# Block sums beside the keys, longer constant products, an added mask and a new order in a sparse-attention and mixture-of-experts kernel

## Chip, cores and metric

The kernel runs on one core of a Trainium2 chip. The metric is device time in microseconds (us). A kernel's time is the median of its runs. The profiled span of a run is some 1.6 us shorter than its time (184.9 against 186.49 in the profiled run of the kernel before).

A run is labelled slow when it is over 1.5% above the fastest run of the same kernel, fast otherwise.

## The reference

There are four sequences (batch entries) of 768 positions. Eight attention heads of 64 channels look at a local window of 31 keys and at 24 block summaries: the maximum of each block's 32 keys and the mean of its values. Then the whole sequence goes to one of eight experts.

```python
k_sum = k.reshape(B, H, nb, block, D).max(axis=3)       # block = 32, nb = 24
v_sum = v.reshape(B, H, nb, block, D).mean(axis=3)
mask_l = np.abs(pos[:, None] - pos[None, :]) < window   # window = 16
scores_s = scale * q @ k_sum.T + np.log(block)          # (einsum, shortened)
a = softmax([where(mask_l, scale * q @ k.T, -1e9), scores_s])
x = a @ [v, v_sum]                                      # -> (B, 768, 512)
# ... mixture of experts, one choice per sequence
logits = x.mean(axis=1) @ w_gate
e = argmax(logits)                                      # one of 8
out = softmax(logits)[e] * (relu(x @ w1[e]) @ w2[e])    # w1 512x1024, w2 1024x512
```

## The kernel before

The kernel carries its own list scheduler. It estimates when each operation can start, picks one by priority, and so fixes the order of instructions on each engine before anything runs. While sequence b+1 is in attention, TensorE works on the expert of sequence b. Three parts matter here.

**The filler.** TensorE's granted clock falls to half for some stretches (0.50 from 30.0 to 40.2 us in the kernel before). The scheduler is written to prevent that: wherever it expects TensorE to have little to do, it puts products of constants into the list. They count as busy in the profiles (22.8 of TensorE's 171.4 busy us in the kernel before).

```python
def keep_warm(self, t, op):
    end = self.work[-1][1]
    idle = t - end
    if t < self.FILL_TO:                       # 45.0
        unit = 0.107 if t < 6.5 else 0.0555
        n = max(0, int((idle - 0.1) / unit))
        past = ...                             # weighted busy time of the last SPAN = 3 us
        thin = self.DENSE * self.SPAN - past - n * unit     # DENSE = 0.5
        if t > 7.0 and thin > 0:
            more = min(int(thin / unit) + 1, 10)
            n += more
    ...
    if self.fill(n): ...

def fill(n):
    ...
    for _ in range(n):
        nc.tensor.matmul(idle[:, 0:128], lhsT=idle_in, rhs=idle_in, start=True, stop=True)
```

**The block sums.** The keys of one query block (96 rows) and the 24 block maxima give 120 rows of scores in one tile `aT`. For the values, the sums of 32 rows are made by a product with a block indicator (`bind`). In sequences 0 to 2 they stay in a tile of their own, `vs`, and a second group of products adds their part. In sequence 3 they are copied by DMA into rows 96 to 119 beside every block's values, and one product with 120 rows does both.

```python
APART = (0, 1, 2)
def av(pr, hf):
    ...
    rows = KW if b in APART else NR            # 96 or 120
    for hh in range(2):
        for jj in range(NH):
            nc.tensor.matmul(ops[...], lhsT=aT[0:rows, hh, ...], rhs=vb[0:rows, pr, j, hh, :], ...)
    if b not in APART:
        return
    for hh in range(2):
        for s in range(NS):                    # six more products per half
            nc.tensor.matmul(ops[:, hh, s, :], lhsT=aT[KW:NR, hh, ...],
                             rhs=vsps[b % 2][KW:NR, pr, hh, :], start=False, ...)
def mk(pr, hf):                                # the mask, on VectorE, after the exponential
    nc.vector.tensor_tensor(out=aT[0:NR], in0=aT[0:NR], in1=mask[...], op=ALU.mult)
```

**The gate and the loads.** The mean of sequence b gives its expert's number, and only then can the two weight matrices be loaded (1 MB each). For sequence 0, w1 comes in two halves, so that the expert can start on the first one. The output leaves through three tiles.

```python
def w1f(half):
    fs = slice(half * (F // 2), (half + 1) * (F // 2)) if b == 0 else slice(0, F)
    nc.gpsimd.dma_start(sb["w1"][:, :, fs], moe_w1[ds(sb["e"], 1)]...)
# letters: A = ScalarE, D = VectorE, per sequence and pair of heads
EK = ("AAAA", "DAAD", "DAAD", "DDDD")          # key copies
EQ = ("ADAD", "AADD", "DDDD", "DADD")          # query copies
KB = ("ADDA", "ADAD", "ADAD", "DAAD")          # key maxima
CAST = ("DDAD", "DDDD", "DDDD", "DDDD")        # casts of the values
o_pool = ctx.enter_context(tc.tile_pool(name="o", bufs=3))
```

The softmax here doesn't subtract the row's maximum and nothing guards it: scores larger than these inputs give would overflow.

## Time and profile before

| | before |
|---|---|
| time, median of 3 runs | 188.2 us (187.96 to 188.72) |
| span of the profiled run | 184.9 us |
| start to gate 0 | 41.3 us |
| gate 0 to first expert product | 9.7 us |
| first expert product to gate 3 | 96.5 us |
| gate 3 to end | 37.4 us |

These four stretches add up to the span. "Gate b" is the start of the gate products of sequence b. Three lines of the page of the kernel before help to read it. The first two are rows of 40 slices of 4.6 us: TensorE's busy tenths, and the mean busy share of the DMA engines. The third is the filler: busy time in us, then nanoseconds of one instruction.

```profile
PE   7898973999999989999999999999999999899991
...
DMA  5999999604999999799999999944100039990052
...
L1031 PE MATMUL third<-idle_in 128*128 128x128 bf16 x273 | 22.8, 244 | 1.4 <-DVE warm L273 1.2
```

The DMA engines are full from the second slice to the seventh, while all inputs of sequence 0 arrive. TensorE's 93% contains 22.8 us of filler, nearly all in the first stretch, just behind gate 0 and behind gate 3. So "busy" says little there, while in the third stretch, where there is no filler, it says that the list itself is the limit.

The page's queue q8, named instruction, moved 18 packets and 0.29 MB, 16 KB each. Such a packet is called a block of instructions here, and its arrival the fetch. A place is a number in TensorE's list of products and weight loads.

### The profile page before, as it was taken

Reading aid. Unit: us, or ns where it says so; the run is one execution under the profiler, and the core shown is the slowest. Engines: PE = TensorE matmul, PEld = TensorE weight load, DVE = VectorE, ACT = ScalarE, POOL = GpSimd, SP = SyncE. Lnnn points to the kernel's source line nnn. Section 1 sums busy time; section 2 is a strip of 40 time slices with the busy share of each in tenths; the row PEclk is TensorE's granted clock in tenths of the full one; section 3 lists DMA queues with packets and bytes.
Section 4 is the critical chain, followed back from the end, with each engine's and each line's share of the span. In section 5 each row is a group of like instructions: output and inputs, shape, how many; then the busy total and the mean of one; then the engine's idle time right before and its main releaser. Section 6 shows DMA issues by size and latency. Waiting matters only on the chain.

```text
span 184.9 us, 5505 instructions
## 1 busy us (share of the span) xinstructions
PE 171.4 (93%) x2365; PEld 109.7 (59%) x2365; DVE 100.3 (54%) x237; ACT 103.2 (56%) x193; POOL 49.1 (27%) x70
## 2 busy tenths in 40 slices
PE   7898973999999989999999999999999999899991
PEld 7787763797666556565566554345666544665440
DVE  5887791569689669699658565103996210000000
ACT  3266581422689567667466746136888743277241
POOL 7998751005930430761123030000000030000000
PEclk9999997569999999999999999999999999999998
DMA  5999999604999999799999999944100039990052
GB/s 103 203 222 172 204 245 207 104 4 43 193 203 203 239 213 155 110 203 191 202 310 261 243 210 184 224 127 175 57 4 2 4 67 222 268 236 5 6 223 113
DMA packets 22792, 29.39 MB, mean 159 GB/s; under 512 B 4944, under 2 KB 16208, under 8 KB 22768
## 3 DMA queue, kind: packets, MB, share of 16 engines
q0 software_dynamic: 15184, 20.58, 63.7%
q1 hardware_dynamic: 7584, 8.47, 15.2%
q8 instruction: 18, 0.29, 0.7%
q14 instruction: 6, 0.05, 0.1%
HBM read 35.67 MB, written 6.29 MB: 227 GB/s over the span
## 4 chain that ended last, share of the span: by engine, by line
PE 75%; DMA 9%; DVE 5%; issue 5%; ACT 3%; POOLq 1%; ACTq 0%; DVEq 0%
PE hps L912 16%; PE hps L943 12%; DMA w_sb<-in_moe_w_dram 9%; PE third L912 8%; PE third L1031 6%; PE third L943 6%; PE ops L614 5%; PE ops L447 4%; PE sc L576 4%; PE tps L650 4%; PE kps L504 3%; PE ops L625 3%; PE tps L530 2%; DVE vblk L348 2%; ACT kT L522 1%
## 5 line engine op out<-in xcount | busy, mean ns | idle before, releaser
L912 PE MATMUL hps<-xT_b,w_sb 128*128 128x512 bf16 (+1 forms) x172 | 33.7, 328 | 1.3 <-issue 0.9
L261 POOL DMA_DIRECT2D v_f<-in_v_dram x30 | 25.1, 848 | 27.1 <-DMA w_sb<-in_moe_w_dram 10.1
L912 PEld LDWEIGHTS <-w_sb 128*128 128x128 bf16 x256 | 23.0, 98 | 15.0 <-DMA w_sb<-in_moe_w_dram 0.9
L587 ACT ACTIVATE aT<-sc 128x768 bf16<-128x768 f32 x32 | 26.0, 811 | 10.1 <-PE sc L576 10.0
L943 PEld LDWEIGHTS <-hT_sb 128*128 128x128 bf16 x192 | 18.0, 98 | 20.6 <-issue 0.4
L943 PE MATMUL hps<-w_sb,hT_sb 128*128 128x512 bf16 x128 | 29.6, 379 | 0.0
L923 ACT ACTIVATE hT_sb<-hps 128x512 bf16<-128x512 f32 (+1 forms) x43 | 20.7, 492 | 8.4 <-PE hps L912 8.1
L1031 PE MATMUL third<-idle_in 128*128 128x128 bf16 x273 | 22.8, 244 | 1.4 <-DVE warm L273 1.2
L833 POOL DMA_DIRECT2D w_sb<-in_moe_w_dram x5 | 4.1, 820 | 73.1 <-PE third L943 42.0
L1031 PEld LDWEIGHTS <-idle_in 128*128 128x128 bf16 x273 | 18.9, 111 | 3.5 <-DVE warm L273 1.2
L591 DVE TENSOR_TENSOR aT<-aT,mask 120x768 bf16<-120x768 bf16 x32 | 17.7, 553 | 3.8 <-ACT aT L587 3.7
L953 ACT ACTIVATE o_sb<-hps,gcol 128x512 f32<-128x512 f32 x16 | 11.0, 686 | 13.4 <-PE hps L943 8.9
L348 DVE CAST vblk<-v_f 64x768 bf16<-64x768 f32 x30 | 17.5, 583 | 1.7 <-DMA v_f<-in_v_dram 1.4
L658 ACT ACTIVATE xT_b<-tps 128x768 bf16<-128x768 bf16 x16 | 12.9, 808 | 8.9 <-PE tps L650 8.8
L912 PE MATMUL third<-xT_b,w_sb 128*128 128x256 bf16 (+1 forms) x84 | 16.9, 324 | 0.2 <-DMA w_sb<-in_moe_w_dram 0.2
L614 PEld LDWEIGHTS <-aT 96*64 96x64 bf16 (+1 forms) x384 | 9.4, 116 | 12.6 <-issue 6.5
L524 DVE COPY kT<-kps 128x960 bf16<-128x960 bf16 (+1 forms) x16 | 11.3, 747 | 9.7 <-PE kps L504 9.7
L640 DVE TENSOR_TENSOR xs<-ops,rv 128x384 bf16<-128x384 f32 x28 | 15.6, 557 | 1.0
L943 PE MATMUL third<-w_sb,hT_sb 128*128 128x512 bf16 x64 | 15.2, 380 | 0.0
L614 PE MATMUL ops<-vblk,aT 96*64 96x65 bf16 (+1 forms) x336 | 11.3, 202 | 3.7 <-issue 3.5
L522 ACT ACTIVATE kT<-kps 128x960 bf16<-128x960 bf16 (+1 forms) x16 | 9.6, 655 | 8.6 <-PE kps L504 6.9
L447 PE MATMUL ops<-vblk,bind 64*32 64x128 bf16 (+1 forms) x84 | 11.9, 286 | 0.9 <-POOL bind L281 0.7
(71 smaller groups left out, 189.8 us busy)
## 6 DMA issues: line engine op xcount, KB each, us to landing
w_sb<-in_moe_w_dram POOLq DMA_DIRECT2D x7, 1024.0 KB, 13.9
out_dram<-o_sb SPq DMA_DIRECT2D x24, 256.0 KB, 5.1
v_f<-in_v_dram POOLq DMA_DIRECT2D x30, 192.0 KB, 10.0
k_nat<-in_k_dram POOLq DMA_DIRECT2D x6, 384.0 KB, 8.4
q_nat<-in_q_dram POOLq DMA_DIRECT2D x6, 384.0 KB, 10.5
vblk<-vblk SPq DMA_DIRECT2D x12, 89.4 KB, 4.8
w_sb<-in_moe_w_dram POOLq DMA_DIRECT2D x2, 512.0 KB, 8.1
k_nat<-in_k_dram POOLq DMA_DIRECT2D x4, 192.0 KB, 5.1
```

What stands on the lines that cost most here:

```text
L261: eng.dma_start(v_f[:, :, h, :], v[b, h].rearrange("(j p) d -> p j d", p=128))
L348: eng.tensor_copy(dst, src)
L447: nc.tensor.matmul(out_ps[p0 : p0 + 32, 0 : n * D], lhsT=bind[:, j, :], rhs=vblks[b % 2][0:QB, ps, j, :, 0:D], start=(j == 0), stop=(j == ...
L587: nc.scalar.activation(aT, sb["sc"][:, :, 0 : NH * QB], ACT.Exp, scale=SCALE)
L591: nc.vector.tensor_tensor(out=aT[0:NR], in0=aT[0:NR], in1=mask[:, hf * NH : (hf + 1) * NH, :] .rearrange("p j c -> p (j c)") .unsqueeze(1) ...
L614: nc.tensor.matmul(ops[(j % 2) * QB : (j % 2 + 1) * QB, hh, jj // 2, :], lhsT=aT[0:rows, hh, jj * QB : (jj + 1) * QB], rhs=vb[0:rows, pr, ...
L640: nc.vector.tensor_tensor(out=sb["xs"][pr][:, hf * NS : (hf + 1) * NS, :, :].rearrange("p s h d -> p h s d"), in0=ops[:, :, :, 0:D], in1=r ...
L658: nc.scalar.activation(sb["xT"][:, pr, :].rearrange("p (j e g) -> p j e g", e=QB // G, g=G), sb["xps"].rearrange("p j g e -> p j e g"), AC ...
L912: nc.tensor.matmul(ps["t"][:, 0 : c1 - c0], lhsT=sb["w1"][:, dt, ft * 128 : (ft + 1) * 128], rhs=sb["xT"][:, dt, c0:c1], start=(dt == 0), ...
L923: nc.scalar.activation(sb["hT"][:, ft, c0:c1], ps["t"][:, 0 : c1 - c0], ACT.Relu)
L943: nc.tensor.matmul(ps["t"], lhsT=sb["hT"][:, ft, st * 128 : (st + 1) * 128], rhs=sb["w2"][:, ft, :], start=(ft == 0), stop=(ft == NFT - 1),)
L1031: nc.tensor.matmul(idle[:, 0:128], lhsT=idle_in, rhs=idle_in, start=True, stop=True)
```

## The change

Its description has five parts: the sums of sequences 1 to 3 are spread beside the keys by VectorE, the filler becomes 512 columns long, the mask of two pairs of heads is added on TensorE before the exponential, three weight buffers, and a new order. The order comes from new letters, priorities, assumed durations and a new sequence of the first loads. The code sets NW = 2, which is what the kernel had, so the third weight buffer is not in it.

```diff
-    FILL_TO = 45.0
+    FILL_TO = 50.0
-    DENSE = 0.5
-    DELAY = {"PE": 1.3, "DVE": 0.6, "ACT": 0.6}
+    DENSE = 0.47
+    DELAY = {"PE": 1.3, "DVE": 0.6, "ACT": 0.4}
+    NW = 2
 ...
+    def setup_shut():                      # 0 inside the window, -30000 outside
+        nc.vector.tensor_tensor(out=both, in0=mask1, in1=mask2, op=ALU.add)
+        shut_of(shut, both.unsqueeze(1).to_broadcast([KW, NJ, QB]))
 ...
-    EK = ("AAAA", "DAAD", "DAAD", "DDDD")
-    EQ = ("ADAD", "AADD", "DDDD", "DADD")
-    KB = ("ADDA", "ADAD", "ADAD", "DAAD")
-    CAST = ("DDAD", "DDDD", "DDDD", "DDDD")
+    EK = ("DADA", "ADAA", "DDAD", "DDDD")
+    EQ = ("DAAD", "ADAD", "ADAD", "DAAA")
+    KB = ("ADAA", "ADAA", "DDDD", "DAAD")
+    CAST = ("DADD", "DDAD", "ADDD", "ADDA")
+    MK = ("DDPP", "DDDD", "DDDD", "DDDD")
-    APART = (0, 1, 2)
+    SUMS = "ASSS"
 ...                                        # first loads: values 4, 6, 5 now ahead of bind (b)
+    for what in "23mp465b7qr":
 ...
+            def spread(c, b=b):
+                nc.vector.tensor_copy(
+                    vblks[b % 2][KW:NR, c, :, :, :],
+                    vsps[b % 2][KW:NR, c, :, :].unsqueeze(1).to_broadcast([NB, NJ, 2, D + 1]),
+                )
 ...                                        # in qk(), for letter P
+            for hh in range(2 * add_shut):
+                nc.tensor.matmul(sc[:, hh, 0 : NH * QB], lhsT=identb[0:KW, :], rhs=shut[...],
+                                 start=True, stop=False)
 ...                                        # four lists of priorities
-        sch.prio = (40.0, 8.0, 12.0, 24.0)[b]
+        sch.prio = (40.0, 30.0, 14.0, 84.0)[b]
 ...
-        for _ in range(n):
-            nc.tensor.matmul(idle[:, 0:128], lhsT=idle_in, rhs=idle_in, start=True, stop=True)
+        for c in [512] * (n // 4) + [n % 4 * 128] * (n % 4 > 0):
+            nc.tensor.matmul(idle[:, 0:c], lhsT=idle_in[:, 0:128], rhs=idle_in[:, 0:c], ...)
```

More of the change, by code (lines that the diff above doesn't have):

```diff
@@ L220 @@
     xt_pool = ctx.enter_context(tc.tile_pool(name="xt", bufs=3))
-    moe_pool = ctx.enter_context(tc.tile_pool(name="moe", bufs=2))
+    moe_pool = ctx.enter_context(tc.tile_pool(name="moe", bufs=NW))
     ht_pool = ctx.enter_context(tc.tile_pool(name="ht", bufs=2))
@@ L241 @@
     kps = kps_pool.tile([128, G, SP + 4], BF16, name="kps")
-    idle_in = const_pool.tile([128, 128], BF16, name="idle_in")
+    idle_in = const_pool.tile([128, 512], BF16, name="idle_in")
     vsps = [const_pool.tile([128, NP, 2, D + 1], BF16, name=f"vs{i}") for i in range(2)]
@@ L267 @@
     mask = const_pool.tile([NR, NJ, QB], BF16, name="mask")
+    shut = const_pool.tile([KW, NJ, QB], BF16, name="shut")
     mask2 = const_pool.tile([KW, QB], BF16, name="mask2")
@@ L316, in setup_later, with shut_of @@
         nc.vector.memset(ones_row, 1.0)
+    both = const_pool.tile([KW, QB], BF16, name="both")
+    def shut_of(dst, src):
+        nc.vector.tensor_scalar(
+            out=dst, in0=src, scalar1=30000.0, scalar2=-30000.0, op0=ALU.mult, op1=ALU.add
+        )
+    def setup_shut():
+        nc.vector.tensor_tensor(out=both, in0=mask1, in1=mask2, op=ALU.add)
+        shut_of(shut, both.unsqueeze(1).to_broadcast([KW, NJ, QB]))
+        shut_of(shut[:, 0, :], mask1)
+        shut_of(shut[QB:KW, NJ - 1, :], mask2[QB:KW])
     def setup_mask():
-        both = const_pool.tile([KW, QB], BF16, name="both")
-        nc.vector.tensor_tensor(out=both, in0=mask1, in1=mask2, op=ALU.add)
         nc.vector.tensor_copy(mask[0:KW], both.unsqueeze(1).to_broadcast([KW, NJ, QB]))
@@ L354, in halo_v @@
         nc.sync.dma_start(vb[QB + 16 : KW, ps, 1:NJ, :, :], vb[QB - 16 : QB, ps, 0 : NJ - 1, :, :])
-    v_loads = [add("SP", 0.5, [], lambda: load_v(0, 0), dma=1.2)]
-    v_loads.append(add("SP", 0.5, [], lambda: load_v(0, 1), dma=1.2, after=v_loads[-1:]))
+    v_loads = {0: add("SP", 0.5, [], lambda: load_v(0, 0), dma=1.2)}
+    v_loads[1] = add("SP", 0.5, [], lambda: load_v(0, 1), dma=1.2, after=[v_loads[0]])
     def load_wg():
@@ L367, in pool_v @@
     def pool_v(h):
-        v_loads.append(add("POOL", 0.75, [], lambda: load_v(0, h), dma=0.65, after=[last]))
-        return v_loads[-1]
+        v_loads[h] = add("POOL", 0.75, [], lambda: load_v(0, h), dma=0.65, after=[last])
+        return v_loads[h]
     qk_loads = {(0, 0): (k0, q0)}
@@ L376, in pool_qk @@
         return kl, add("POOL", 0.65, [], lambda: load_qk(0, *hs, (1,)), dma=1.35, after=[kl])
-    last = pool_v(2)
-    last = pool_v(3)
-    last = keep_setup = add("POOL", 0.9, [], setup_keep, after=[last])
-    qk_loads[0, 1] = pool_qk(1)
-    last = qk_loads[0, 1][1]
-    last = bind_setup = add("POOL", 1.2, [], setup_bind, after=[last])
-    last = pool_v(4)
-    last = pool_v(5)
-    last = pool_v(6)
-    last = pool_v(7)
-    qk_loads[0, 2] = pool_qk(2)
-    last = qk_loads[0, 2][1]
-    qk_loads[0, 3] = pool_qk(3)
-    last = qk_loads[0, 3][1]
-    wg_load = add("SP", 0.5, v_loads[1:2], load_wg, dma=0.3)
+    for what in "23mp465b7qr":
+        if what == "m":
+            last = keep_setup = add("POOL", 0.9, [], setup_keep, after=[last])
+        elif what == "b":
+            last = bind_setup = add("POOL", 1.2, [], setup_bind, after=[last])
+        elif what in "pqr":
+            pair = 1 + "pqr".index(what)
+            qk_loads[0, pair] = pool_qk(pair)
+            last = qk_loads[0, pair][1]
+        else:
+            last = pool_v(int(what))
+    wg_load = add("SP", 0.5, [v_loads[1]], load_wg, dma=0.3)
     vb_setup = add("DVE", 0.7, [], lambda: setup_vb(0))
@@ L395 @@
     ones_setup = add("DVE", 0.9, [], setup_ones, after=[dve_setup])
-    mask_setup = add("DVE", 1.2, [keep_setup, ones_setup], setup_mask)
+    shut_setup = add("DVE", 1.0, [keep_setup], setup_shut)
+    sch.prio = 40.0 if "D" in MK[0] else 0.0
+    mask_setup = add("DVE", 1.0, [shut_setup, ones_setup], setup_mask)
     sch.prio = 0.0
@@ L421, in v_ops @@
                     "ACT" if on_act else "DVE",
-                    1.65 if on_act else 1.05,
+                    1.7 if on_act else 1.17,
                     [loads[2 * c], loads[2 * c + 1]] + prev + [vb_setup if b == 0 else later_setup],
@@ L444, in vs @@
                 st["ps"] = out_ps = ops_pool.tile([128, 512], FP32, name="ops")
-                p0 = KW if b in APART else 0
+                p0 = 0 if SUMS[b] == "B" else KW
                 for j in range(NJ):
@@ L456, in ev @@
                 dst, src = (
-                    (vsps[b % 2][KW:NR], st["ps"][KW:NR])
-                    if b in APART
-                    else (vsbs[b % 2], st["ps"][0:NB])
+                    (vsbs[b % 2], st["ps"][0:NB])
+                    if SUMS[b] == "B"
+                    else (vsps[b % 2][KW:NR], st["ps"][KW:NR])
                 )
@@ L472, in bc @@
                         )
+            def spread(c, b=b):
+                nc.vector.tensor_copy(
+                    vblks[b % 2][KW:NR, c, :, :, :],
+                    vsps[b % 2][KW:NR, c, :, :].unsqueeze(1).to_broadcast([NB, NJ, 2, D + 1]),
+                )
             o_vs = add("PE", 0.7 if b == 0 else 2.7, [casts[c] for c in cs] + deps + [bind_setup], vs, lat=0.2, dense=0.45)
@@ L479, in v_ops @@
             o_bc = o_ev
-            if b not in APART:
+            if SUMS[b] == "B":
                 o_bc = add("SP", 2.4, [o_ev], bc, dma=1.6)
             for c in cs:
+                if SUMS[b] == "S":
+                    o_bc = add("DVE", 0.68, [o_ev] + prev, lambda c=c, f=spread: f(c))
                 done.append([halos[c], o_bc])
@@ L571, in qk @@
             sc = sb["sc"] = sc_pool.tile([128, 2, 512], FP32, name="sc")
+            add_shut = MK[b][pr] == "P"
+            for hh in range(2 * add_shut):
+                nc.tensor.matmul(
+                    sc[:, hh, 0 : NH * QB],
+                    lhsT=identb[0:KW, :],
+                    rhs=shut[:, hf * NH : (hf + 1) * NH, :].rearrange("p j c -> p (j c)"),
+                    start=True,
+                    stop=False,
+                )
             for jj in range(NH):
@@ L579, in qk @@
                         rhs=sb["qT"][pr][rs, j, :],
-                        start=True,
-                        stop=True,
+                        start=not add_shut,
+                        stop=not add_shut or jj == NH - 1,
                         tile_position=(hh * D, 0),
@@ L609, in av @@
             )
-            rows = KW if b in APART else NR
+            rows = KW if SUMS[b] == "A" else NR
             for hh in range(2):
@@ L617, in av @@
                         rhs=vb[0:rows, pr, j, hh, :],
-                        start=(b not in APART or (hh == 0 and jj < 2)),
-                        stop=(b not in APART),
+                        start=(SUMS[b] != "A" or (hh == 0 and jj < 2)),
+                        stop=(SUMS[b] != "A"),
                     )
-            if b not in APART:
+            if SUMS[b] != "A":
                 return
@@ L676, in add_T @@
             o_ek = add(
-                *(("ACT", 1.25) if EK[b][pr] == "A" else ("DVE", 1.45)), [o_tk] + td,
+                *(("ACT", 1.25) if EK[b][pr] == "A" else ("DVE", 1.5)), [o_tk] + td,
                 lambda: ek(pr, EK[b][pr] == "A"),
@@ L690, in add_T @@
                 o_km = add("DVE", 0.95, [o_ek], lambda: km(pr))
-            o_kb = add(*(("ACT", 0.45) if KB[b][pr] == "A" else ("DVE", 0.4)), [o_km] + td, lambda: kb(pr))
+            o_kb = add(*(("ACT", 0.45) if KB[b][pr] == "A" else ("DVE", 0.26)), [o_km] + td, lambda: kb(pr))
             ts["first"], qts["first"] = o_ek, o_eq
@@ L699, in add_QK @@
             sl, sd = sch.slot("sc", 1)
-            o_qk = add("PE", 0.35, deps + sd, lambda: qk(pr, hf), lat=0.2, dense=0.45)
+            by_pe = MK[b][pr] == "P"
+            o_qk = add(
+                "PE", 0.85 if by_pe else 0.35, deps + sd + [shut_setup] * by_pe, lambda: qk(pr, hf),
+                lat=0.2, dense=0.6 if by_pe else 0.45,
+            )
             ts["readers"].append(o_qk)
@@ L705, in add_QK @@
             as_["first"] = o_ex
+            if by_pe:
+                return as_, o_ex
             o_mk = add("DVE", 0.57, [o_ex, mask_setup], lambda: mk(pr, hf))
@@ L711, in add_AV @@
             os_, od = sch.slot("mps", 2) if spare(hf) else sch.slot("ops", 1)
-            o_av = add("PE", 0.38 if b not in APART else 0.62, [o_mk] + v_ready[b][pr] + od, lambda: av(pr, hf), lat=0.2, dense=0.4)
+            o_av = add("PE", 0.38 if SUMS[b] != "A" else 0.62, [o_mk] + v_ready[b][pr] + od, lambda: av(pr, hf), lat=0.2, dense=0.4)
             as_["readers"] = [o_av]
@@ L1003 @@
     for b in range(B):
-        sch.prio = (40.0, 0.0, 4.0, 0.0)[b]
+        sch.prio = (40.0, 20.0, 4.0, 4.0)[b]
         sequence, xsl, x_ops = attention(b)
@@ L1010 @@
             rest()
-        sch.prio = (40.0, 8.0, 12.0, 24.0)[b]
-        w = gate(b, x_ops, moe_last.get(b - 2, []), order_pool)
+        sch.prio = (40.0, 30.0, 14.0, 84.0)[b]
+        w = gate(b, x_ops, moe_last.get(b - NW, []), order_pool)
         sch.prio = 0.0
@@ L1015 @@
         if nxt < B:
-            sch.prio = (0.0, 0.0, 4.0, 0.0)[nxt]
+            sch.prio = (0.0, 10.0, 60.0, -2.0)[nxt]
             casts, bcs = v_ops(nxt, vl)
@@ L1021 @@
             rest()
-        sch.prio = (0.0, 12.0, 0.0, 0.0)[b]
+        sch.prio = (-12.0, 12.0, 6.0, 0.0)[b]
         moe_last[b] = moe(b, w, xsl)
@@ L1029, in fill @@
         idle = third_pool.tile([128, 512], FP32, name="third")
-        for _ in range(n):
-            nc.tensor.matmul(idle[:, 0:128], lhsT=idle_in, rhs=idle_in, start=True, stop=True)
+        for c in [512] * (n // 4) + [n % 4 * 128] * (n % 4 > 0):
+            nc.tensor.matmul(idle[:, 0:c], lhsT=idle_in[:, 0:128], rhs=idle_in[:, 0:c], start=True, stop=True)
         return True
```

## The prediction

> **What bounds the kernel now.** I read the table of engine shares first, then the same table cut into stages, the chain that ended last, TensorE's timeline, and last the groups by shape. The page's first lines, and its row of granted clock:
>
> ```profile
> span 184.9 us, 5505 instructions
> PE 171.4 (93%) x2365; PEld 109.7 (59%) x2365; DVE 100.3 (54%) x237; ACT 103.2 (56%) x193; POOL 49.1 (27%) x70
> ...
> PEclk9999997569999999999999999999999999999998
> ```
>
> TensorE (PE) is busy for 93%, VectorE (DVE) and ScalarE (ACT) for little over half. But one fortieth is 4.6 us, and in slices 7 to 9 TensorE had about half its clock. Cut at the gate products of sequence 0 (41.4), the first expert product (51.0), the gate of sequence 3 (147.5), and the ends of sequence 2's expert and of the last weight wait:
>
> ```profile
> 0.00:41.40 41.40, 34.27 (x638) 29.50 (x639) 28.11 (x71) 19.72 (x32) 22.74 (x37) 0.88 0.88 163
> 41.40:51.00 9.60, 9.39 (x167) 6.68 (x166) 7.37 (x18) 4.06 (x9) 6.58 (x8) 1.00 0.82 120
> 51.00:147.50 96.50, 95.02 (x1364) 56.18 (x1364) 63.90 (x142) 63.36 (x124) 18.14 (x23) 1.00 0.85 168
> 147.50:157.20 9.70, 9.52 (x51) 4.36 (x51) 0.90 (x7) 3.83 (x7) 1.63 (x2) 1.00 0.66 139
> 157.20:159.90 2.70, 2.28 (x38) 2.10 (x37) 0.00 (x0) 0.47 (x1) 0.00 (x0) 1.00 1.09 269
> 159.90:184.90 25.00, 20.93 (x112) 10.87 (x112) 0.00 (x0) 11.74 (x23) 0.00 (x0) 0.97 0.48 128
> ```
>
> Columns: stretch, length, busy us of PE, PEld, DVE, ACT, POOL, clock, DMA share, GB/s. From 51.0 to 147.5 TensorE is busy 95.0 of 96.5 us: what leaves its list there leaves the time. The first 41.4 us are different, as constant filler products (third<-idle_in) count as busy. The chain shows what holds them up:
>
> ```profile
> 27.44 0.18 PE ops L614 x3
> 27.61 3.08 issue
> 30.70 0.44 PE ops L614 x9
> ...
> 40.00 1.41 PE third L1031 x22
> 41.40 0.29 PE ops L802 x8
> ...
> 43.85 7.13 DMA w_sb<-in_moe_w_dram
> ```
>
> TensorE stops for 3.08 us inside a run of twelve equal products, waiting for nothing that the profile sees. In half-microsecond windows its clock falls from 1.00 to 0.50 at 30.0 and returns at 40.2. The gate's result then starts a weight load of 7.1 us. So the start of the saturated stretch is gate 0 plus 9.6 us.
>
> [...] (1) [...] the page's q8 moved 18 packets, 0.29 MB, 16 KB each. [...] TensorE's unexplained stops (0.41, 3.08, 0.39 and 0.85 us at 21.9, 27.6, 59.7 and 67.4) stand at places 702, 957, 1962 and 2216 of its list, so 255, 1005 (four times 251) and 254 apart, about one block each [...]. (2) [...] from 26.0 to 30.0 TensorE was busy for 0.7 us. (3) [...] eight expert products took 1.73 us, 216 each. (4) [...] 768 elements took 356 ns as a copy of the mask, 553 as its multiplication.
>
> **The change, part by part.** The groups that I price it by:
>
> ```profile
> L625 PE MATMUL ops<-vs,aT 24*128 24x65 bf16 x120 | 7.4, 195 | 0.0
> L591 DVE TENSOR_TENSOR aT<-aT,mask 120x768 bf16<-120x768 bf16 x32 | 17.7, 553 | 3.8 <-ACT aT L587 3.7
> L348 DVE CAST vblk<-v_f 64x768 bf16<-64x768 f32 x30 | 17.5, 583 | 1.7 <-DMA v_f<-in_v_dram 1.4
> L568 DVE COPY kT<-kmx 128x288 bf16<-128x288 bf16 x8 | 2.0, 252 | 0.1
> L321 DVE COPY mask<-both 96x768 bf16<-96x768 bf16 x1 | 0.4, 356 | 0.0
> ```
>
> *Block sums.* For sequences 1 and 2 the separate products with the sums go: 2 x 8 groups of six. A group takes 0.287 us from start to start in TensorE's timeline, so 16 x 0.287 = **4.6 us, all on the saturated path**. The sums join the main product, with 120 rows in place of 96; sequence 3 has that form already, and its group of twelve takes 0.31 us with either. Sequence 3 swaps its copies by DMA for VectorE's. VectorE pays 12 copies of 24x1560. From 288 elements in 252 ns and 768 in 356, a line gives 0.52 us; I take 0.55, so 6.6 us.
>
> *Engine letters.* VectorE: four cast pairs fewer (4 x 2 x 0.583 = -4.7), two key copies more (2 x 1.49 = +3.0), four query copies fewer (-2.2), four mask multiplications fewer (-2.2), mask constants and a wider fill of the constant (+1.3), spreads +6.6: **+1.8**. ScalarE: eight casts more at 0.848 (+6.8), two key copies fewer (2 x 1.31 = -2.6), four query copies more at 0.807 (+3.2): **+7.4**. Both stay near 60% of the span, so neither becomes the bound on average.
>
> *Mask on TensorE.* Two pairs of sequence 0: eight products of 384 columns, 0.16 us each by (3), +1.3, in the unsaturated first part. It takes 0.55 us off each of four latency chains there.
>
> *Longer constants.* Four 128-column fillers took about 0.24 us warm, one of 512 should take 0.216. What matters is the list: gate 0 stands at place 1271 before, 1041 after.
>
> *Three buffers.* The diff sets NW = 2, as before: nothing changes.
>
> *Order up to gate 0.* Adding TensorE's groups of the new list at the old durations (fillers 0.107 us per 128 columns up to 6.2, then 0.06) gives 22.7 us at pair 3's key transposes and about 33.5 at gate 0; with short idles 34.5. The old list without the stop (3.1) and with half of some 9.5 busy us at half clock back (4.7) also gives 33.6. The fetch still has to keep up. Block 3 came 6.3 us after block 2 was entered (16.0 to 22.3), block 4 another 8.4 later. In the new list place 447 falls at about 19.3 and place 702 at 24.4, 5.1 apart; 957 follows after some 5.6. At the old delays that is a stop of 1 to 3 us at each, 2 to 5 in all, partly under waits for other engines[...]. I put gate 0 at 37 instead of 41.4: **-4.4 us**.
>
> *Between gate 0 and the first expert product* the load stays 9.6 us. TensorE's new list has one key and one query transpose group and two score groups more there (2 x 0.46 + 2 x 0.29 = 1.5), in place of fillers: **-1.5**.
>
> *Tail.* Gate 3 stands after one of sequence 2's six output products in both lists, five follow, then filler. The last load needs 12.4 us from the gate, TensorE has some 9.5: the hole of about 2.9 us and the 37.4 us from gate 3 to the end stay.
>
> *New waits.* Gate 2 has some 15 us of TensorE work behind it instead of 25, against a load of 2.7 + 9.0; gate 1 some 16 against 13.8. Enough, but tight; DVE, already 4.9 of 5 us busy from 55 to 60, gets the spreads there. I allow **+1.4**.
>
> Sum: -4.6 - 4.4 - 1.5 + 1.4 = -9.1, so 188.2 - 9.1 = 179.1, call it **179.0 us**.
>
> **Rivals.** *A: the fetch stop comes back in full and takes the clock.* For it: the DMA share is still about 1.0 up to 34 us, and the sections above are close to the old stop. Against: fewer instructions, and two shorter stops. Then gate 0 stays near 41 and the time is about 183. *B: VectorE or ScalarE becomes the bound between 51 and 147.* For it: the busy stretch at 55 to 60, and a fixed order in which TensorE waits. Against: 66% busy each over that stretch. It would eat 3 to 5 us: 182 to 184. *C: a weight load of sequence 1 or 2 is no longer hidden:* 2 to 4 us, about 182. *D: all goes to plan without stops:* gate 0 at 34.5, 176 or a little less.
>
> **Range and chances.** Only removed products are nearly certain (4.6 us, alone 2.4%). D and a well-packed middle give 174.5, A or B with nothing moved ahead 183.8. Two of the bad cases together would be needed to stay above 184.4. Faster by over 2%: 0.89; within: 0.09; slower: 0.02.
>
> **What would show it.** Gate 0 near 37, with clock rows free of a half-speed stretch, and issue stops near places 702 and 957 of the list. No products with the sums in sequences 1 and 2, spreads near 0.55 us. First expert product 9.6 us after gate 0. From there to gate 3 about 90 to 92 us instead of 96.5. The tail still 37 us with its filler. The prediction is wrong if the clock drops again before 40 us, if TensorE idles over 3 us more in the middle, or if the spreads take 1.5 us.

## The result

| | before | after |
|---|---|---|
| time, median | 188.3 us (187.96 to 188.72, 4 runs) | 181.7 us (180.33 to 182.56, 4 runs) |
| ratio of fast runs | | 0.9642, 95% interval 0.9573 to 0.971 |

A ratio here is the mean time of one kernel's fast runs over that of the other's fast runs of the same rounds, so it is not quite the ratio of the medians. The kernel after is 6.6 us faster by the medians, and the output is correct. The profiled runs differ by 4.3 us only, because the profiled run of before (186.49) was a quick one for that kernel.

The page of the kernel after begins like this; the last line is the queue of instruction blocks, with packets and MB (16 KB a packet again).

```profile
span 180.6 us, 4939 instructions
PE 170.7 (95%) x2083; PEld 96.2 (53%) x2083; DVE 103.2 (57%) x240; ACT 110.3 (61%) x201; POOL 48.5 (27%) x70
...
PEclk9999955557999999999999999999999999999999
...
q8 instruction: 16, 0.26, 0.6%
```

TensorE has 282 products fewer, but its busy time fell by 0.7 us only. The row of the granted clock tells why: the halved stretch is now five slices long instead of three. The cut into the four stretches, with columns as in the prediction, is this.

```profile
0.00:43.81 43.81, 39.83 (x520) 23.90 (x520) 31.29 (x75) 20.66 (x32) 22.44 (x37) 0.77 0.85 158
43.81:53.54 9.73, 9.73 (x180) 5.75 (x179) 8.09 (x19) 7.69 (x16) 6.83 (x9) 1.00 0.84 127
53.54:143.52 89.98, 88.48 (x1218) 50.43 (x1212) 62.89 (x140) 65.95 (x124) 17.59 (x23) 1.00 0.86 174
143.52:180.60 37.08, 32.65 (x173) 16.10 (x172) 0.90 (x7) 16.04 (x30) 1.65 (x2) 0.99 0.58 142
```

| stretch | before | after | difference | predicted |
|---|---|---|---|---|
| start to gate 0 | 41.3 | 43.8 | +2.5 | -4.4 |
| gate 0 to first expert product | 9.7 | 9.7 | 0.0 | 0 |
| first expert product to gate 3 | 96.5 | 90.0 | -6.5 | -4.7 (= -4.6 - 1.5 + 1.4) |
| gate 3 to end | 37.4 | 37.1 | -0.3 | 0 |

The middle gave more than was predicted, and the first stretch lost where a gain was predicted. How much it lost is less sure than the table looks, because the profiled run of before was a quick one. By the medians, taking off the 1.6 us and what follows gate 0 (143.6 and 136.8 us), gate 0 would stand at some 43.1 us before and 43.3 after. This is an estimate. So the 2.5 us belong to this pair of runs; what both ways show is that the predicted gain of 4.4 us did not come. What filled the middle, by the time from one product's start to the next one's:

| first expert product to gate 3, us | before | after |
|---|---|---|
| expert, first and second product | 33.7 + 23.3 | 33.8 + 23.6 |
| products with the sums apart | 4.6 (96) | 0 |
| query and key transposes | 4.8 + 3.8 | 3.7 + 3.6 |
| scores | 6.2 | 5.6 |
| output of attention, its transposes | 7.5 + 4.7 | 7.2 + 4.4 |
| making the sums | 5.5 | 5.5 |
| idle | 1.4 | 1.4 |

The spreads by VectorE and the product that takes their rows, as groups of the kernel after (instructions, busy us, nanoseconds of one, idle before):

```profile
L645 PE MATMUL ops<-vblk,aT 120*64 120x65 bf16 x288 | 9.1, 199 | 0.2 <-DVE xs L671 0.2
...
L489 DVE COPY vblk<-vs 24x1560 bf16<-24x1560 bf16 x12 | 6.5, 561 | 0.2
```

A product with 120 rows takes 199 ns, one with 96 rows took 203 ns before: the added rows cost nothing here. Twelve spreads take 561 ns each.

The first stretch needs a closer look. The clock's records show half speed from 22.7 to 43.2 us, which is 20.48 us. Before, it was 30.0 to 40.2, 10.24 us, half as long. In the experiments below half speed lasted 6.8 us (sums_apart), 17.1 (short_fill_first) and 23.9 (short_fill). To within 0.1 us these are six, three, two, five and seven times 3.41 us, which is called a window of the clock here. TensorE's timeline of the kernel after, just ahead of it (start, us from first start to last end, and in brackets the idle time with what ended it):

```profile
17.24 0.21 PE L461 MATMUL ops<-vblk,bind 64*32 64x128 bf16 x1
18.08 0.80 PE L461 MATMUL ops<-vblk,bind 64*32 64x128 bf16 x11 [0.62 <-DVE vblk L363]
18.81 0.35 PE L607 MATMUL sc<-qT,kT 64*128 64x64 bf16 x12
19.09 0.39 PE L1068 MATMUL third<-idle_in 128*128 128x512 bf16 x1
20.05 0.86 PE L461 MATMUL ops<-vblk,bind 64*32 64x128 bf16 x12 [0.57 <-DVE vs L475]
```

TensorE waits for casts and sums on VectorE, and the list has just one filler product there. In windows, the same run shows what came of it:

```profile
17.50:20.00 2.50, 1.40 (x24) 1.03 (x24) 2.42 (x4) 0.80 (x1) 2.26 (x4) 1.00 1.20 183
...
22.70:43.20 20.50, 20.41 (x254) 12.64 (x252) 11.91 (x27) 11.02 (x20) 2.74 (x4) 0.50 0.67 131
```

From 17.5 to 20.0 TensorE was busy for 1.40 of 2.50 us, with VectorE at 2.42. Three microseconds later the clock went to 0.50. From then on TensorE was busy for 20.41 of 20.50 us, as its products took longer (twelve score products 0.43 us from their start to the next group's at 26.7, against 0.28 at 12.2), and still the clock stayed down. No stop without a visible cause was longer than 0.35 us: the stop that cost 3.08 us before did not come here.

The tail is unchanged. The chain of the kernel after at gate 3 (start, us, what) has the same weight load as before, 10.03 us against 10.07:

```profile
143.59 0.29 PE ops L839 x8
...
145.79 10.03 DMA w_sb<-in_moe_w_dram
155.82 0.05 issue
155.86 1.90 PE hps L949 x8
```

### The profile page after: what moved, and what is told of

Same layout as the page of the kernel before. It is cut to its first block, busy times and chain, and to the rows that moved or that the text cites. A ratio compares the mean times of both kernels' runs of the same rounds, so it can differ in the third digit from the quotient of the medians.

```text
span 180.6 us, 4939 instructions
## 1 busy us (share of the span) xinstructions
PE 170.7 (95%) x2083; PEld 96.2 (53%) x2083; DVE 103.2 (57%) x240; ACT 110.3 (61%) x201; POOL 48.5 (27%) x70
## 4 chain that ended last, share of the span: by engine, by line
PE 63%; DMA 18%; DVE 10%; issue 3%; ACT 1%; POOL 1%; POOLq 1%; ACTq 0%; DVEq 0%
PE hps L949 12%; PE hps L980 12%; DMA q_nat<-in_q_dram 9%; PE third L949 6%; PE third L980 6%; DMA w_sb<-in_moe_w_dram 6%; DMA v_f<-in_v_dram 4%; PE sc L607 4%; PE ops L461 3%; PE ops L645 3%; PE tps L681 3%; PE third L1068 3%; DVE vblk L363 3%; PE kps L526 3%; PE tps L552 2%
## 5 line engine op out<-in xcount | busy, mean ns | idle before, releaser
L949 PE MATMUL hps<-xT_b,w_sb 128*128 128x512 bf16 (+1 forms) x172 | 33.1, 328 | 0.4 <-DMA w_sb<-in_moe_w_dram 0.4
L262 POOL DMA_DIRECT2D v_f<-in_v_dram x30 | 25.2, 851 | 26.6 <-DMA w_sb<-in_moe_w_dram 11.6
L949 PEld LDWEIGHTS <-w_sb 128*128 128x128 bf16 x256 | 22.8, 98 | 14.2 <-DMA w_sb<-in_moe_w_dram 0.8
L1068 PE MATMUL third<-idle_in 128*128 128x512 bf16 (+2 forms) x79 | 22.4, 421 | 1.9 <-DVE warm L275 1.6
L622 DVE TENSOR_TENSOR aT<-aT,mask 120x768 bf16<-120x768 bf16 x28 | 15.5, 556 | 3.0 <-ACT aT L618 2.6
L546 DVE COPY kT<-kps 128x960 bf16<-128x960 bf16 (+1 forms) x20 | 14.1, 745 | 2.3 <-PE kps L526 2.3
L363 DVE CAST vblk<-v_f 64x768 bf16<-64x768 f32 x22 | 13.2, 601 | 2.4 <-issue 2.1
L1068 PEld LDWEIGHTS <-idle_in 128*128 128x128 bf16 x79 | 7.6, 111 | 11.9 <-issue 5.8
L645 PEld LDWEIGHTS <-aT 120*64 120x64 bf16 (+1 forms) x384 | 9.6, 119 | 7.9 <-issue 3.4
L990 ACT ACTIVATE o_sb<-third,gcol 128x512 f32<-128x512 f32 x8 | 5.5, 688 | 12.2 <-PE third L980 9.2
L361 ACT ACTIVATE vblk<-v_f 64x768 bf16<-64x768 f32 x10 | 8.5, 846 | 6.6 <-DMA v_f<-in_v_dram 6.6
```

Of the source, the lines that this page charges most:

```text
L262: eng.dma_start(v_f[:, :, h, :], v[b, h].rearrange("(j p) d -> p j d", p=128))
L363: eng.tensor_copy(dst, src)
L645: nc.tensor.matmul(ops[(j % 2) * QB : (j % 2 + 1) * QB, hh, jj // 2, :], lhsT=aT[0:rows, hh, jj * QB : (jj + 1) * QB], rhs=vb[0:rows, pr, ...
L949: nc.tensor.matmul(ps["t"][:, 0 : c1 - c0], lhsT=sb["w1"][:, dt, ft * 128 : (ft + 1) * 128], rhs=sb["xT"][:, dt, c0:c1], start=(dt == 0), ...
L990: nc.scalar.activation(ps["o"], ps["t"], ACT.Copy, scale=sb["gcol"][:, 0:1])
L1068: nc.tensor.matmul(idle[:, 0:c], lhsT=idle_in[:, 0:128], rhs=idle_in[:, 0:c], start=True, stop=True)
```

## The experiments

All twelve kernels gave correct results. They ran in three batches of four, each batch on one chip; the kernel before had medians of 187.08, 187.13 and 186.71 us in them (7 runs each). Every other median is of 4 runs. A ratio is always to the kernel before.

### 1. sums_apart: the new order with the old sums

```diff
-    SUMS = "ASSS"
+    SUMS = "AAAB"
```

> The changed kernel with its block sums handled as before (separate products in sequences 0 to 2, copies by DMA in sequence 3), all else as changed. Theory, removed products: the first part keeps its list, so gate 0 stays at about 43.8 us and the clock falls there as in the changed kernel; from the first expert product to gate 3 the 16 groups of 0.287 us come back, so 94 to 95 us instead of 90.0, and the time is about 186. Rival, the new order and letters made the gain: the time stays within 1.5 us of 181.7.

Measured: 189.18 us (185.95 to 195.06), ratio 1.0126 (1.0035 to 1.0218), two of four runs slow. This undoes the spreads alone: the priorities stay, and so does the list up to gate 0. Its two last stretches:

```profile
48.50:146.31 97.81, 96.19 (x1323) 55.77 (x1319) 56.86 (x128) 65.67 (x124) 17.54 (x23) 1.00 0.82 164
146.31:184.40 38.09, 33.88 (x179) 16.69 (x178) 0.90 (x7) 15.93 (x30) 1.65 (x2) 1.00 0.57 138
```

The middle is 97.8 us (94 to 95 were expected), 7.8 more than after and 1.3 more than before. It holds the products with the sums again (4.6 us), and one more output product of an expert (25.2 us of the expert's second products against 23.6), whose place behind gate 3 was taken by filler (5.3 us instead of 2.2). So the new order without the spreads gains nothing in the middle.

Its first stretch was a surprise. Although the list there is that of the kernel after, the clock was at half speed for two windows (21.1 to 27.9), not six, and gate 0 came at 38.8 instead of 43.8. That is 5.0 us for 13.7 us more of half speed, 0.37 us lost for each. The same list can therefore have either fate. At this rate the list would reach gate 0 at some 36 us with the clock up all the time (43.8 - 0.37 x 20.5), which is an estimate.

### 2. warm: a dozen more constant products in the thin place

```diff
-        if self.fill(n):
+        extra = 4 if 14.0 < t < 24.0 else 0
+        if self.fill(n + extra):
```

> The changed kernel with one more 512-column constant product ahead of each group of TensorE that its scheduler places between 14 and 24 us (some 12 more, 2.6 us of TensorE time, where TensorE stood idle for about 2 us); the order of all real work is unchanged. Theory, a thin stretch costs the clock: the clock stays at 1.00 until gate 0, gate 0 comes at 36 to 38 us instead of 43.8, and the time is 175 to 177. Rival, the clock falls for another reason: the half-speed stretch stays, gate 0 comes at 44 to 46, the time is 182 to 184.

Measured: 177.57 us (176.84 to 178.33), ratio 0.9518 (0.9457 to 0.958), all four runs fast with a mean clock of 0.999 to 1.000. The kernel after had 0.940 to 0.958 in its four runs. The order of everything else is the same. The two windows of the result, in this run:

```profile
17.50:20.00 2.50, 2.25 (x29) 1.22 (x28) 2.42 (x4) 0.48 (x1) 1.78 (x3) 1.00 1.16 184
...
22.70:43.20 20.50, 20.35 (x401) 13.13 (x401) 16.19 (x40) 15.08 (x28) 5.32 (x7) 1.00 0.80 149
```

From 17.5 to 20.0 TensorE is now busy for 2.25 instead of 1.40 us, the clock stays at 1.00, and 401 products pass between 22.7 and 43.2 instead of 254. Gate 0 comes at 38.2; from gate 0 to the end it takes 137.0 us, as in the kernel after (136.8). So the clock is the whole difference between these two profiles, and products added at 14 to 24 us keep it up. The gain is 4.1 us by the medians, which are of different batches, and 2.3 us by the ratios to the kernel before (0.9518 against 0.9642).

### 3. old_first: sequence 0 as before

```diff
-    EK = ("DADA", ...   EQ = ("DAAD", ...   KB = ("ADAA", ...   CAST = ("DADD", ...   MK = ("DDPP", ...
+    EK = ("AAAA", ...   EQ = ("ADAD", ...   KB = ("ADDA", ...   CAST = ("DDAD", ...   MK = ("DDDD", ...
-    for what in "23mp465b7qr":
+    for what in "23mpb4567qr":
```

> The changed kernel with the letters, the order of loads and the mask of sequence 0 as before; the list from gate 0 on is that of the changed kernel. Theory, the gain lies after gate 0 and the new first part lost time: gate 0 at 41 us or earlier, the stretch from first expert product to gate 3 at 90 us, total 177 to 179.5. Rival, the new first part is better and only its clock was bad luck: gate 0 at 43 us or later, total 181 or more.

Measured: 176.8 us (174.86 to 177.52), ratio 0.9477 (0.9411 to 0.9542), mean clocks 0.986 to 1.000. From gate 0 on the list is that of the kernel after. The profile's first stretch, and the window compared above:

```profile
0.00:36.10 36.10, 30.96 (x515) 18.80 (x516) 30.16 (x76) 21.48 (x35) 23.12 (x37) 1.00 0.98 187
```

```profile
22.70:43.20 20.50, 19.57 (x413) 12.95 (x413) 18.16 (x45) 16.47 (x30) 7.38 (x10) 1.00 0.96 175
```

Gate 0 comes at 36.1, the earliest of all runs, and the rest takes 137.1 us. The new letters and loads of sequence 0 thus cost time, and by the estimate of number 1 (some 36 us at full clock) they cost it through the clock alone; the gain of the change lies behind gate 0. The later kernels that say "old_first" start from here.

### 4. short_fill: the kernel after with short constants

```diff
-        for c in [512] * (n // 4) + [n % 4 * 128] * (n % 4 > 0):
+        for c in [128] * n:
```

> The changed kernel with its constant products cut to 128 columns again, same columns at the same places. Theory, the amount of filler counts and not its form: the clock falls between 20 and 26 us here too, and the time is within 1% of 181.7. Rival, the long form is at fault: no half-speed stretch or a much shorter one, 177 or less. Second rival, fewer instructions kept the fetch from stopping TensorE: stops of 1 to 3 us without a cause come back before gate 0 and the time is 183 to 185.

Measured: 182.22 us (177.97 to 185.54), three of four runs slow, no ratio. The profiled run, a slow one, had half clock from 20.0 to 43.9 and gate 0 at 45.0. No stop near place 950 can be seen in either kernel's profile: at half speed TensorE comes there late, and a block of instructions had landed by then (in short_fill it landed at 28.4 us and TensorE came at 31.9; in the kernel after 34.9 and 38.2; how this is read is told under number 8). So this run is inconclusive on the length of the filler.

### 5. short_fill_first: short constants where the clock holds

The edit of number 4 in old_first.

> The version with the old first part (176.8), its constant products cut to 128 columns. Its list is longer, and place 950 comes with pair 3's first score products at about 28 us instead of the fillers at 32. Theory, the fetch: a stop without a cause at about place 950, 1.5 to 3.5 us long, gate 0 at 39 to 42 us instead of 36 to 38.7, total 2 to 5 us longer. Rival, the form of the filler plays no part: no stop over 0.5 us, total within 1% of 176.8.

Measured: 182.55 us (179.64 to 183.7), three of four runs slow (clocks 0.947 to 0.981), no ratio. That is 5.8 us above old_first, on another chip whose kernel before was 0.4 us quicker. Fast runs alone give less: the one fast run took 179.64 us, the three of old_first 176.15 on average, 3.5 us apart. The profiled run has two stops without a visible cause, 0.60 us at place 700 and 1.19 us at place 954 of TensorE's list, and five windows of half clock (26.3 to 43.4). Gate 0 came at 44.2; the rest took 136.7 us as ever. Long constants seem worth having in this list, by that one fast run. How much of it is the stops and how much the clock is not separated by this run.

### 6. long_fill_only: the kernel before with long constants

```diff
-    idle_in = const_pool.tile([128, 128], BF16, name="idle_in")
+    idle_in = const_pool.tile([128, 512], BF16, name="idle_in")
-        for _ in range(n):
+        for c in [512] * (n // 4) + [n % 4 * 128] * (n % 4 > 0):
```

> The kernel before with constant products of 512 columns, nothing else. Theory, fewer instructions let the fetch keep up: place 957 of TensorE's list falls two groups before gate 0 rather than six, the stop of 3.1 us is gone or under 1.5 us, the clock stays up or falls for one or two windows, gate 0 comes at 36 to 39 us instead of 41.3, total 1.3 to 2.7% below before. Rival, the stop comes from the load of the DMA queues at 27 to 31 us whatever the list: a stop of about 3 us again, gate 0 at 41, total as before.

Measured: 182.26 us (181.82 to 185.49), ratio 0.9762 (0.9625 to 0.9899). The page's row of granted clock:

```profile
PEclk9999998599999999999999999999999999999999
```

The stop of 3.08 us is gone: the list has some 195 filler products fewer (2170 weight loads against 2365), so TensorE needs fewer instructions for the same work. The clock fell at nearly the same place all the same (29.9), but for two windows instead of three. Gate 0 came at 37.6, and the rest took 143.3 us, against 143.6 before. This part alone gives 3.7 us by the profiled gate 0, all of it in the first stretch; by the ratio it gives 4.5 us, with an interval of 1.9 to 7.0. The stop near place 950 is gone: TensorE came there at 32.8, and the block had landed at 30.8. Another of 0.95 us stands later, at 81.3 us.

### 7. sums_only: the kernel before with the spreads

Only `SUMS = "ASSS"`, the spreads and the 120-row products; order, letters, loads and filler as before.

> The kernel before with the block sums of the change alone (spread by VectorE, joined to the main product), its old priorities and letters. Its list keeps only 2 of sequence 2's 6 output products behind gate 3 (5 in the kernel before and in the changed one) and 110 fillers. Theory, removed products pay only where the order brings gate 3 forward: gate 0 at 41.3 as before, first expert product to gate 3 about 96 to 97 us (4.6 us of products gone, three output products of 1.75 moved in), tail 37.4, total within 1.5 us of the kernel before. Rival, the sums alone pay 4.6 us: total 2.4% below before.

Measured: 190.52 us (188.56 to 191.24), ratio 1.0188 (1.0057 to 1.0319). Removing 4.6 us of saturated TensorE work made the kernel slower (1.0057 is the low end of the interval; the class is unclear at 2%). Its two last stretches, then TensorE's timeline behind gate 3:

```profile
52.00:149.78 97.78, 94.27 (x1274) 54.91 (x1294) 69.96 (x153) 64.54 (x126) 18.14 (x23) 1.00 0.84 170
149.78:189.60 39.82, 32.73 (x246) 19.57 (x248) 0.90 (x7) 13.98 (x27) 1.63 (x2) 0.96 0.50 116
```

```profile
149.77 0.35 PE L810 MATMUL ops<-wg_sb,pooled 128*1 128x8 f32 x8
...
153.93 6.30 PE L1039 MATMUL third<-idle_in 128*128 128x128 bf16 x110
163.47 3.00 PE L920 MATMUL hps<-xT_b,w_sb 128*128 128x512 bf16 x7 [3.24 <-DMA w_sb<-in_moe_w_dram]
```

The products with the sums are gone from the middle, but the scheduler put three more output products of sequence 2's expert (28.2 us of second products against 23.3) ahead of gate 3. So gate 3 did not come earlier, and two output products were left to cover its load. The rest of the load is 6.3 us of filler and 3.2 us of idling, and the clock fell there too. What leaves the list is only a gain here if gate 3 comes earlier by it. From gate 0 to the end the four cases took 143.6 us (before), 147.4 (spreads alone, with a fall of the clock in the tail), 145.6 (the whole change without spreads) and 136.8 (the whole change).

### 8. first_mask: old_first with the added mask

```diff
-    MK = ("DDDD", ...
+    MK = ("DDPP", ...
```

> The version with the old first part, with the mask of two pairs of sequence 0 on TensorE added back (8 more products of 384 columns, 4 mask multiplications of VectorE fewer). Theory, it takes 0.55 us off a chain of latencies at most and adds 1.3 us of TensorE: gate 0 at 35 to 37 us against 36.1, total within 1% of the version without it (176.8), unless the clock falls. Rival, this mask is what loses the first part's time: gate 0 at 38 or later with the clock up.

Measured: 176.13 us (173.37 to 181.88) against 176.8 for old_first, ratio 0.937 (0.9196 to 0.9544), two runs slow. The added mask moves the time by less than the runs scatter. With it the scheduler also put other work ahead of gate 0 in a new order, so this is not the mask alone. The profiled run (slow) has one stop; TensorE's timeline:

```profile
31.14 0.19 PE L645 MATMUL hps<-vblk,aT 96*64 96x65 bf16 x1
33.45 0.38 PE L645 MATMUL hps<-vblk,aT 96*64 96x65 bf16 x11 [2.12 <-issue]
```

Again TensorE stops inside a group of twelve equal products, for 2.12 us and for no visible reason, at about place 950 of its list. Stops stand there in seven profiles, of five lists that differ up to there: 3.08 us before (957), 0.82 in sums_apart, 1.85 in sums_only, 2.12 here, 1.60 in split_last, 1.19 in short_fill_first and 1.14 in three_buffers, at places 946 to 957 (counted from the recorded products and weight loads, of which a trace can lack a few: the middle of long_fill_only has 1346 products beside 1365 loads). A wait in the program would move with the program; these stops kept their place to within 11.

The traces hold firmer evidence than the place. The packets of the instruction queue (q8), the blocks of 16 KB, are recorded. In the kernel before one ran from 27.83 to 29.16 us, and the stop ended at 30.70; here one ran from 30.62 to 31.97, and the stop ended at 33.45. All 13 stops of over 0.35 us without a visible cause, in all 14 profiles, ended 1.27 to 1.71 us after such a block had landed. In old_first the block landed at 31.03 and TensorE's product at the place began at 32.57, without such a stop. So the stops are read here as waits for instructions that landed late.

### 9. three_buffers: the weight buffers of the description

```diff
-    NW = 2
+    NW = 3
```

> The version with the old first part, with three weight buffers instead of two (the words of the change speak of three, its code keeps two); TensorE's list is identical. Theory, a weight load waits for its gate and never for a buffer: no difference, total within 1% of 176.8 but for the first part's clock. Rival, a load waits for its buffer: the tail or the stretch before gate 3 gets shorter by over 1 us.

Measured, on old_first: 175.29 us (174.67 to 178.49), ratio 0.9357 (0.9267 to 0.9446). Its middle is 89.7 us and its tail 37.3, against 90.0 and 37.4 (profiled values of old_first). A third buffer brings nothing that can be told from scatter: no sign here that a load waits for a buffer.

### 10. split_last: the last load in halves

On old_first: w1 of the last sequence comes in two halves, as that of the first, and no filler after 100 us.

```diff
-            n = int((idle - 1.2) / unit)
+            n = 0 if t > 100.0 else int((idle - 1.2) / unit)
 ...                                        # in w1f()
+            for fs in [slice(0, F // 2), slice(F // 2, F)] if b == B - 1 else [fs]:
                 nc.gpsimd.dma_start(sb["w1"][:, :, fs], moe_w1[...])
```

> The version with the old first part; sequence 3's first weights are loaded in two halves, and the filler in front of its expert is left out; all other order unchanged. Theory, the hole behind gate 3 (3.0 us of filler and idling) is the wait for the whole of that load: the first half lands about 8 us after gate 3, under the 9.5 us of output products, so the tail falls from 37.5 to about 34.7 and the total from 176.8 to 174. Rival, two smaller loads take as long as one to give their first half, or the clock falls in the gap: tail 37 or more.

Measured: 177.87 us (175.58 to 178.63), two runs slow, no ratio. The tail is 37.1 us: nothing gained. The expert did start at once (147.9), but then TensorE stood for 2.9 us. The chain of the run:

```profile
142.96 0.70 ACT o_sb L991
143.66 0.02 issue
143.68 7.34 DMA out_dram<-o_sb
...
151.12 0.70 ACT o_sb L991
151.82 0.04 issue
151.86 1.02 PE hps L950 x4
```

The wait has changed its name. An output tile written at 143.0 takes 7.34 us to reach memory beside the weight loads (the median store of the kernel before took 5.1); ScalarE needs that tile again before it can free the accumulator that the next expert product wants.

### 11. split_store: and six output tiles

```diff
-    o_pool = ctx.enter_context(tc.tile_pool(name="o", bufs=3))
+    o_pool = ctx.enter_context(tc.tile_pool(name="o", bufs=6))
```

The scheduler's own count of these tiles stays at three; only the memory behind them grows.

> The split-load version with six output tiles in place of three. In the split-load run the first product of sequence 3's expert started at once (147.9), then TensorE waited 2.9 us for an accumulator bank that ScalarE could not empty, because an output tile was still being stored (7.3 us beside the weight loads). Theory, that wait took the place of the load's: with six tiles it goes, gate 3 to the end takes 34 to 35 us instead of 37.1, and the total is 173 to 175.5 depending on the first part's clock. Rival, the second half of the load is the next wait: tail 36 to 37.

Measured: 172.52 us (172.25 to 173.12), ratio 0.9226 (0.9158 to 0.9293), all four runs fast. The last stretch:

```profile
136.59:170.70 34.11, 30.18 (x160) 15.24 (x162) 0.90 (x7) 16.06 (x30) 2.38 (x3) 0.99 0.65 154
```

and the chain where the hole was:

```profile
144.64 1.46 PE hps L981 x6
146.09 1.80 PE hps L950 x8
147.90 0.44 PE third L950 x4
```

The tail is 34.1 instead of 37.1 us, and the expert's products follow the output products without a gap. This is the fastest version, and it beats both kernels.

### 12. all_together: split_store with more filler early

```diff
-        if self.fill(n):
+        if self.fill(n + (2 if 14.0 < t < 30.0 else 0)):
```

> The version of the six output tiles, with 256 more columns of filler ahead of each group between 14 and 30 us, to hold the clock: theory, no half-speed window before gate 0, gate 0 at 36.5 to 38 us in every run, so a narrower range of times than its twin without them, and a median of 172.5 to 174.5. Rival, the added filler costs more than the clock it saves: median above its twin's.

Measured: 174.36 us (174.2 to 175.28), ratio 0.9326 (0.9255 to 0.9397). The clocks are 0.997 to 1.000, against 0.986 to 0.996 without. But 1.8 us were lost: in this list one window of half speed costs less than the filler that prevents it. What helped the kernel after (warm) hurts here.

## Why the prediction was right or wrong

The total was right: 179.0 predicted, 181.7 measured, within 174.5 to 183.8, and faster by over 2%. It came out of one step that failed and some that were too cautious, and that the miss was no larger is in part luck. By the medians the failed step was off by some 4.6 us (+0.2 by the estimate above, where -4.4 was predicted); the middle gave back 1.8 and the tail 0.3. The base was mixed, too: the savings were read from a run of 186.49 us and taken off a median of 188.2. Taken off their own run, they give 177.4.

**Block sums: right in size, incomplete in reason.** The products that left the middle took 4.6 us, as predicted, and the spreads took 0.561 us where 0.55 was assumed. But the prediction called the removal a gain "all on the saturated path". The experiments sums_only (ratio 1.0188) and sums_apart (1.0126) show that neither the removal nor the new order is a gain by itself, with these lists. Removal leaves a hole in a fixed list, and the gain is there only when the order lets gate 3 move into it.

**"Engine letters": right.** VectorE's busy time rose by 2.9 us (1.8 predicted), ScalarE's by 7.1 (7.4).

**"Between gate 0 and the first expert product": right.** The load stayed 9.7 us. The work that moved into it took 1.0 us of query transposes, 0.6 of scores and 0.3 of key transposes from the middle, 1.9 against the predicted 1.5. These are the groups that the prediction named.

**"New waits": a size that was off.** 1.4 us were allowed; TensorE's idle time in the middle stayed at 1.4. The lone new wait that stands out is 1.15 us for VectorE at 74.6, and others fell. Rivals B and C, an engine as the new bound and an exposed load of sequence 1 or 2, did not come.

**"Tail": right.** 37.4 became 37.1 us.

**"Order up to gate 0": wrong.** The step put gate 0 at 37 instead of 41.4 and had stops of the fetch as the way it could fail; rival A had them take the clock too, with gate 0 near 41. No such stop came. The clock fell without one, earlier and for twice as long, and gate 0 came at 43.8 in the profile. The step priced the list at full speed, and at full speed it was about right: warm, with the clock up and a dozen products more, has gate 0 at 38.2. The prediction took the fetch stop for the only thing that could thin TensorE's work. Even in the old order the stop was not needed: in long_fill_only the clock fell at 29.9 with the stop gone. That the stop took the clock was the author's estimate, from the one fall at 30.0 inside the stop of 27.6 to 30.7; no run shows it to be the cause. That half of the busy time at half clock would come back was an estimate as well; number 1 gives 0.37 us for each us of half speed. The prediction did not ask where in the new list TensorE would wait for VectorE, and VectorE is 9.5 of 10 us busy between 10 and 20 us. The warning was among its own signs ("wrong if the clock drops again before 40 us").

**"Longer constants": listed, not priced.** The prediction looked at them for the fetch alone. In the kernel before they give 3.7 us by themselves (long_fill_only), in old_first 3.5 us by the one fast run (short_fill_first). They take 194 of the 282 products off TensorE's list (96 more are the products with the sums, and the mask adds 8). In long_fill_only the stop near place 950 went, but four other profiles with long constants still have it (0.82 to 2.12 us). In the kernel after this gain was eaten by the half clock, as far as the profiles show.

**"Mask on TensorE": right as neutral.** first_mask and old_first agree within 0.7 us. **"Three buffers": right.** The code has none, and adding one changes nothing.

What stays open: which measure of TensorE's activity the clock follows, if it follows one. In the kernel after it fell behind a window (19.3 to 22.7) with TensorE 83% busy by the profile (2.84 of 3.41 us), and came back behind one (39.8 to 43.2) with TensorE busy throughout, mostly with constant products. In old_first it stayed up in the profiled run although its idle time up to gate 0 is larger (3.5 us against 2.2), and in sums_apart the list of the kernel after got off with two windows. And in first_mask it stayed up behind a window (14.6 to 18.0) with TensorE only 56% busy (1.91 of 3.40 us), and in old_first behind 1.02 busy us of 2.50 (15.0 to 17.5). Neither busy share nor idle time tells these apart. Leaving out the transposes does not help either: the other products of the window of the kernel after streamed some 4,080 columns, and in the kernel before the window 23.2 to 26.6 had some 3,750 and kept its clock. Nor is it shown why the kernel after got a low clock in all four of its runs and sums_apart a range from 0.953 to 0.981. That added products in the thin place prevent the fall is shown for this list (warm, mean clocks 0.999 to 1.000 against 0.940 to 0.958); a rule for how many is not.

## What to carry to other kernels

Cut the span at the events that start loads, and price a change in each piece by what ends that piece: after gate 0 every variant with the new list and the old tail took 136.7 to 137.1 us in its profile, so the scatter lay ahead of it. In this statically ordered list, work that left the busy engine paid only when something on the end path moved forward into the hole (ratio 1.0188 with the spreads alone, 0.9642 with the new order as well); undo each half of such a change to see it. Filler counted as busy (22.8 us in the kernel before), so read the granted clock beside the busy share, and when one wait is removed, look for the buffer that takes its place, as the output tile did here (a store of 7.34 us cost TensorE 2.9 us).
